# A tenth of the exponentials on VectorE, scores in rounds of four heads, one shared PSUM bank: attention with a gated feed-forward on one core

## The chip, the cores and the metric

The kernel runs on one core of a Trainium2 chip. The time is that of one execution in device microseconds, the median of three runs. One execution was also taken by the hardware profiler. A core has five engines that work through queues of their own and wait for one another by semaphores: TensorE (PE; PEld are its weight loads), VectorE (DVE), ScalarE (ACT), GpSimd (POOL) and SyncE (SP, which only starts transfers here). The on-chip memory SBUF and the matmul memory PSUM have 128 partitions. PSUM has eight banks of 512 fp32 columns.

## The reference: what is computed

The inputs are bf16: `x` (2048 × 640), `wqkv` (640 × 1920), `wo` (640 × 640), `w_gate` and `w_up` (640 × 1728), `w_down` (1728 × 640). With 32 heads of 20 columns:

```
xn = layernorm(x)
q, k, v = heads of xn @ wqkv                         # 32 heads, 20 columns
s  = concat over heads of softmax(q k^T / sqrt(20)) v   @ wo
h  = sigmoid(xn @ w_gate) * (xn @ w_up)              # 1728 columns
out = x + s * silu(h @ w_down)
```

The scores of a head are a 2048 × 2048 matrix, so that the whole softmax takes 32 × 2048 × 2048 exponentials. In banks of 128 keys × 512 queries these are 2048 banks. All the rest of the work is small beside that on ScalarE, but it is not on TensorE.

## The kernel before

**Setup (L133 to L308).** `x` is loaded, normalised (statistics on VectorE), transposed on TensorE into `xnT`; the first keys, values and queries are made. Weights are padded so that each head holds 32 columns, the 20 of the head and one at place 0 that carries constants. In `kT_all` that place is 1 (`e0`), and in the values `v_all` too, so that the matmul with the values also gives the softmax's denominator. In the queries it carries minus an upper bound of the scores: `q_abs` (L103) makes the absolute value of q from PSUM in two VectorE instructions, a copy to bf16 (L105) and a bitwise AND on it (L107), and a matmul with `bound` (L96, L97; made from the maxima of k, L100) sums it into place 0. So the exponential never overflows, and no maximum over the scores is taken.

**Passes and chunks.** The work is 32 passes, `steps`: four chunks of 512 queries, and for each the eight groups of four heads. A pass has 16 tiles of 128 keys × 4 heads = 64 banks of scores. `scores` (L631 to L641) makes one bank per matmul (L638): four heads sit in four row bands of 32 of the array. The banks are cut into chunks of three and two in turn, `scA` and `scB` in PSUM; ScalarE takes each chunk's exponential in one instruction (L680) and writes `pA` or `pB` in SBUF as bf16. `pv` (L647 to L667) multiplies two key tiles × four heads of probabilities with the values, eight matmuls (L661) into the one bank `oacc`, the heads in four column bands. At a pass's end `normalise` (L494) copies `oacc` out (`oev`, L497), and sends the denominators through DRAM to spread them over the partitions (L498, L505, L510 and four broadcasts L515, all in GpSimd's queue), with a reciprocal (L509) between; GpSimd multiplies (L520).

**The fill.** All other matmuls are cut into jobs that run between the scores: `k_job`, `v_job`, `q_job` for later passes (L336 to L363), `gateup_job` (L377) with its tanh on ScalarE (L396) and product on VectorE (L410), `down_job` (L415; copy L427, tanh L431, product L435), `out_job` (L460; L456 on VectorE, L458 on GpSimd), and `part_job` (L476). They share two banks, `misc`. sigmoid and silu are made from tanh.

**The order.** The program is written out in one order, and each engine's queue follows it. Per chunk the loop L675 to L706 emits the exponential, the tanhs and products that are due (`defer`, counted in chunks), the scores of the next chunk, a `pv` where it is due, and as much fill as fits: `room` is ScalarE's time for the chunk less TensorE's for the rest, at 216 ns per matmul of 512 columns (`MM`) and 100 ns per change of kind (`SWITCH`); `credit` grows by the work that is left over the chunks that are left (`quota`). PSUM: three banks `scA`, two `scB`, two `misc`, one `oacc`.

```
pt = wk.tile([P, n, 512], BF16, tag=("pA", "pB")[ci % 2], bufs=3, name=("pA", "pB")[ci % 2])
nc.scalar.activation(out=pt, in_=sc, func=ACT.Exp)
```

**The end (L709 to L764).** After the last exponential come the last `pv`, the last normalising by matmuls, the last two groups of `wo` and the stores.

Of the kernel before, what the change touches and what calls it, by code (L numbers as in the profile page):

```python
# [20 lines left out]
CHUNK = (3, 2)  # L21
# [3 lines left out]
def kernel(  # L25
# [24 lines left out]
    scale = float(Dh) ** -0.5  # L50
# [27 lines left out]
    v_all = persist.tile([P, TT, HEAD, 32], BF16, name="v_all")  # L78
# [5 lines left out]
    ep = early.enter_context(tc.tile_pool(name="early", bufs=1))  # L84
# [3 lines left out]
    def k_matmuls(ps, g, c):  # L88
        for kd in range(KD):
            nc.tensor.matmul(ps, lhsT=wkp[:, kd, GH * g:GH * g + GH, :].rearrange("p h e -> p (h e)"),  # L90
                             rhs=xnT[:, kd, c * 512:(c + 1) * 512],
                             start=(kd == 0), stop=(kd == KD - 1))
            yield
# [9 lines left out]
    def q_abs(ps):  # L103
        absq = wk.tile([P, QC], BF16, tag="absq", bufs=2, name="absq")
        nc.vector.tensor_copy(out=absq, in_=ps)  # L105
        bits = absq.bitcast(mybir.dt.uint16)
        nc.vector.tensor_scalar(out=bits, in0=bits, scalar1=0x7FFF, scalar2=None, op0=ALU.bitwise_and)  # L107
        return absq

    def v_matmuls(ps, tt, h):  # L110
        for kd in range(KD):
            nc.tensor.matmul(ps[:, 0:HALF], lhsT=xnT[:, kd, tt * P:(tt + 1) * P],  # L112
                             rhs=wv[:, kd, h * HALF:(h + 1) * HALF],
                             start=(kd == 0), stop=(kd == KD - 1))
            yield

    def v_dst(tt, h):
        return v_all[:, tt, h * HH:(h + 1) * HH, 1:1 + Dh]

    def q_matmuls(ps, qc, g):  # L120
        for kd in range(KD):
            nc.tensor.matmul(ps, lhsT=wqp[:, kd, GH * g:GH * g + GH, :].rearrange("p h e -> p (h e)"),  # L122
                             rhs=xnT[:, kd, qc * QC:(qc + 1) * QC],
# [8 lines left out]
    v_done = set()  # L132
    with tc.tile_pool(name="setup", bufs=1) as sp, \  # L133
# [29 lines left out]
        nc.vector.memset(v_all[:, :, 0:HH, 1 + Dh:32], 0.0)  # L163
# [7 lines left out]
        for j in range(GH):  # L171
            nc.gpsimd.memset(e0[32 * j:32 * j + 1, :], 1.0)
            nc.gpsimd.memset(esum[32 * j:32 * j + 32, 32 * j:32 * j + 1], -1.0)
# [41 lines left out]
        def k_mm(c):  # L215
            kps[c] = ps0.tile([P, 512], FP32, tag="k", bufs=2, name="ps_k")
            for _ in k_matmuls(kps[c], 0, c):
                pass
# [5 lines left out]
        def v_mm(t):  # L224
            vps[t] = ps0.tile([P, 512], FP32, tag="v", bufs=2, name="ps_v")
            for _ in v_matmuls(vps[t], t, 0):
                pass

        def v_evict(t):
            nc.scalar.activation(out=v_dst(t, 0), in_=vps[t][:, 0:HALF].rearrange("p (h e) -> p h e", e=Dh),  # L230
                                 func=ACT.Copy)
            v_done.add((t, 0))
# [3 lines left out]
        def q_mm():  # L236
            first["ps"] = ps0.tile([P, 512], FP32, tag="q", bufs=1, name="ps_q")
            for _ in q_matmuls(first["ps"], 0, 0):
# [6 lines left out]
        def q_evict():  # L245
            qT = wk.tile([P, QC], BF16, tag="qT", bufs=3, name="qT")
            nc.scalar.activation(out=qT, in_=first["ps"], func=ACT.Copy, scale=scale)
# [55 lines left out]
        nc.gpsimd.memset(v_all[:, :, HH:HEAD, 1 + Dh:32], 0.0)  # L303
# [9 lines left out]
    def misc(name):  # L313
        return psum.tile([P, 512], FP32, tag="misc", bufs=2, name=name)


    SWITCH, MM = 100.0, 216.0
    oTs = {}
    later = []
    slot = [0]  # L320

    def defer(n, fn):
        later.append((slot[0] + n, fn))

    def run_later(everything=False):
        while True:
            due = [x for x in later if everything or x[0] <= slot[0]]
            if not due:
                return
            for x in due:  # L330
                later.remove(x)
            for x in due:
                x[1]()


    def k_job(g, c):  # L336
        ps = misc("ps_k")
        for _ in k_matmuls(ps, g, c):
            yield MM
        dst = kT_all[:, g, c * 512:(c + 1) * 512]  # L340
        nc.vector.tensor_scalar(out=dst, in0=ps, scalar1=e0[:, 0:1], scalar2=None, op0=ALU.add)
        k_max(dst, g, c)
        if c == 3:
            k_bound(g)

    def v_job(tt, h):
        ps = misc("ps_v")
        for _ in v_matmuls(ps, tt, h):
            yield HALF / 2.4 + 3
        nc.vector.tensor_copy(out=v_dst(tt, h), in_=ps[:, 0:HALF].rearrange("p (h e) -> p h e", e=Dh))  # L350
        v_done.add((tt, h))

    def q_job(qc, g):
        ps = misc("ps_q")
        for _ in q_matmuls(ps, qc, g):
            yield MM
        absq = q_abs(ps)
        yield None
        nc.tensor.matmul(ps, lhsT=bound[:, g, :], rhs=absq, start=False, stop=True, skip_group_check=True)
        qT = wk.tile([P, QC], BF16, tag="qT", bufs=3, name="qT")  # L360
        nc.vector.tensor_scalar(out=qT, in0=ps, scalar1=scale, scalar2=None, op0=ALU.mult)
        qTs[qc, g] = qT
        yield MM  # L363
# [3 lines left out]
    def load_glu(c, kf):  # L367
        fsz, f0 = fsz_list[kf], kf * P
        wg = glu[0].tile([P, KD, P], BF16, tag="wg", bufs=3, name="wg")
        nc.sync.dma_start(out=wg[:, :, 0:fsz], in_=B_w_gate[:, f0:f0 + fsz].rearrange("(kd p) f -> p kd f", p=P))  # L370
        wu = glu[0].tile([P, KD, P], BF16, tag="wu", bufs=3, name="wu")
# [3 lines left out]
    hTs = {}  # L375

    def gateup_job(c, kf):  # L377
        fsz = fsz_list[kf]
        n = c * NFT + kf + 2
# [6 lines left out]
        t0 = c * QC  # L386
        psg = misc("psg")
        for kd in range(KD):
            nc.tensor.matmul(psg[0:fsz, :], lhsT=wg[:, kd, 0:fsz], rhs=xnT[:, kd, t0:t0 + QC],  # L389
                             start=(kd == 0), stop=(kd == KD - 1))  # L390
            yield MM
        tnh = wk.tile([P, QC], BF16, tag="tnh", bufs=2, name="tnh")
        done = []

        def gate():
# [397 lines left out]
```

## Time and profile before

| what | value |
|---|---|
| three runs | 1080.61, 1086.87, 1092.41 us; median 1086.87 |
| profiled execution | span 1079.7 us from the first to the last instruction; no other time is shown for it |
| mean granted TensorE clock | 0.929 |
| busy | PE 84%, ACT 92%, DVE 24%, POOL 22% of the span |
| first and last start of an exponential of the scores | 52.38 and 1050.96 us |
| chain that ended last | ACT 57%, issue 20%, PE 17%, DVE 5% |
| the two largest groups | L680 on `scA`, 410 times; L680 on `scB`, 409 times |

A row of groups names line, engine, operation, output and input with their shapes, how often, then busy us, the mean ns of one, and the engine's idle time just before them with what ended it. An ACT duration of 1590 ns for three banks does not mean that the next can start 1590 ns later: successive instructions overlap by some 0.25 us, and starts show the rate. PEclk is the clock that TensorE was granted, in tenths of full speed.

### The profile page before, as it was taken

What the parts mean: (1) busy time and instruction counts of PE and PEld (TensorE: products, weight loads), DVE (VectorE), ACT (ScalarE), POOL (GpSimd) and SP (SyncE); (2) the same over time, 40 slices, a digit from 0 to 9 for tenths busy, and PEclk for the clock granted to TensorE, in tenths of its full rate; (3) what the DMA queues carried; (4) which work ended last, traced back from release to release, by engine and by line L of the source; (5) the groups of instructions that cost most, each with busy time, mean ns of one, the idle gap of its engine ahead of it and who ended that gap; (6) DMA issues with size and microseconds to landing.
All of it is one profiled execution on the core that took longest, in us unless ns stands there. A gap on an engine that the chain in (4) does not pass through costs nothing.

```text
span 1079.7 us, 15225 instructions
## 1 busy us (share of the span) xinstructions
PE 906.9 (84%) x5968; PEld 295.3 (27%) x5968; DVE 259.3 (24%) x477; ACT 990.1 (92%) x934; POOL 232.5 (22%) x368
## 2 busy tenths in 40 slices
PE   4599999999998888888888987888887988889983
PEld 2232332322232322222321222222232332223332
DVE  7533444511122211111111111111111111111212
ACT  4497999999998999999988999999999999999990
POOL 6601111111122411111220321111111331111142
PEclk9798999999998999999965899889998999999995
DMA  5110000332111221111120212111011122210000
GB/s 188 26 30 12 11 12 9 111 73 65 36 54 66 67 54 39 43 39 30 42 66 14 65 42 48 42 42 41 27 60 41 42 67 54 48 32 12 12 23 24
DMA packets 92327, 48.79 MB, mean 45 GB/s; under 512 B 78724, under 2 KB 86820, under 8 KB 92256
## 3 DMA queue, kind: packets, MB, share of 16 engines
q1 hardware_dynamic: 83776, 33.03, 12.2%
q0 software_dynamic: 8480, 14.80, 4.5%
q8 instruction: 46, 0.75, 0.3%
q14 instruction: 25, 0.20, 0.1%
HBM read 40.74 MB, written 7.06 MB: 44 GB/s over the span
## 4 chain that ended last, share of the span: by engine, by line
ACT 57%; issue 20%; PE 17%; DVE 5%; POOL 0%; POOLq 0%; ACTq 0%; DVEq 0%
ACT pA L680 27%; ACT pB L680 24%; ACT tnh L396 4%; PE scA L638 3%; PE scB L638 3%; PE oacc L661 2%; PE psd L424 2%; PE psg L389 2%; ACT td L431 1%; DVE stats L187 1%; PE ps_v L112 1%; DVE absq L107 1%; PE pss L467 1%; PE psu L403 1%; PE ps_k L90 1%
## 5 line engine op out<-in xcount | busy, mean ns | idle before, releaser
L680 ACT ACTIVATE pA<-scA 128x1536 bf16<-128x1536 f32 x410 | 652.0, 1590 | 24.8 <-PE scA L638 24.6
L680 ACT ACTIVATE pB<-scB 128x1024 bf16<-128x1024 f32 x409 | 476.0, 1164 | 8.1 <-PE oacc L661 5.1
L638 PEld LDWEIGHTS <-kT_all 32*128 32x128 bf16 x2048 | 119.9, 91 | 376.4 <-issue 354.4
L638 PE MATMUL scB<-qT,kT_all 32*128 32x512 bf16 x818 | 170.9, 398 | 57.3 <-ACT pB L680 43.7
L638 PE MATMUL scA<-qT,kT_all 32*128 32x512 bf16 x1230 | 168.4, 399 | 48.4 <-ACT pA L680 37.8
L661 PE MATMUL oacc<-pA,v_all 128*32 128x512 bf16 x1230 | 167.3, 407 | 1.0 <-ACT pA L680 1.0
L661 PE MATMUL oacc<-pB,v_all 128*32 128x512 bf16 x818 | 165.7, 407 | 0.2 <-ACT pB L680 0.2
L498 POOL DMA_DIRECT2D den_dram<-oev x31 | 18.2, 588 | 476.1 <-DVE oev L497 476.1
L410 DVE SCALAR_TENSOR_TENSOR hT<-tnh,psu 128x512 bf16<-128x512 bf16 (+1 forms) x56 | 38.4, 686 | 275.7 <-PE psu L403 139.2
L424 PE MATMUL psd<-wd,hT 128*128 128x320 bf16 x448 | 99.0, 323 | 0.5 <-ACT tnh L396 0.5
L389 PE MATMUL psg<-xnT,wg 128*128 128x512 bf16 (+1 forms) x280 | 93.9, 399 | 4.9 <-ACT tnh L396 4.9
L403 PE MATMUL psu<-xnT,wu 128*128 128x512 bf16 (+1 forms) x280 | 86.7, 391 | 0.0
L515 POOL DMA_DIRECT2D rl<-rec_dram x124 | 61.5, 501 | 48.0 <-DMA rec_dram<-den 45.0
L122 PE MATMUL ps_q<-xnT,wqp 128*128 128x512 bf16 x160 | 52.2, 400 | 1.4 <-ACT tnh L396 1.4
L424 PEld LDWEIGHTS <-hT 128*128 128x128 bf16 x448 | 34.0, 100 | 69.9 <-issue 60.3
L520 POOL TENSOR_TENSOR oT<-oev,rl 128x512 bf16<-128x512 f32 x31 | 39.2, 1264 | 58.8 <-DMA rl<-rec_dram 50.9
L661 PEld LDWEIGHTS <-v_all 128*32 128x32 bf16 x2048 | 31.4, 95 | 68.1 <-issue 68.1
L90 PE MATMUL ps_k<-xnT,wkp 128*128 128x512 bf16 x160 | 48.4, 391 | 1.5 <-DVE mk_all L100 1.4
L427 DVE COPY d<-psd 128x320 f32<-128x320 f32 x32 | 15.7, 491 | 129.2 <-PE psd L424 129.2
L497 DVE COPY oev<-oacc 128x512 f32<-128x512 f32 x31 | 21.4, 692 | 100.7 <-PE oacc L661 100.6
L467 PE MATMUL pss<-wo_pad,oT 128*128 128x320 bf16 x192 | 42.4, 325 | 0.0
L396 ACT ACTIVATE tnh<-psg 128x512 bf16<-128x512 f32 (+1 forms) x56 | 40.9, 731 | 0.0
(97 smaller groups left out, 532.9 us busy)
## 6 DMA issues: line engine op xcount, KB each, us to landing
wg<-in_B_w_gate_dram SPq DMA_DIRECT2D x52, 160.0 KB
wu<-in_B_w_up_dram SPq DMA_DIRECT2D x52, 160.0 KB
rl<-rec_dram POOLq DMA_DIRECT2D x124, 64.0 KB, 2.3
gq_dram<-d POOLq DMA_DIRECT2D x12, 320.0 KB, 2.4
gqr<-gq_dram SPq DMA_DIRECT2D x12, 320.0 KB
xr<-in_A_x_dram SPq DMA_DIRECT2D x16, 160.0 KB
wd<-in_B_w_down_dram SPq DMA_DIRECT2D x1, 2080.0 KB
out_dram<-ot POOLq DMA_DIRECT2D x12, 160.0 KB, 2.7
```

What stands on the lines that cost most here:

```text
L90: nc.tensor.matmul(ps, lhsT=wkp[:, kd, GH * g:GH * g + GH, :].rearrange("p h e -> p (h e)"), rhs=xnT[:, kd, c * 512:(c + 1) * 512], start= ...
L122: nc.tensor.matmul(ps, lhsT=wqp[:, kd, GH * g:GH * g + GH, :].rearrange("p h e -> p (h e)"), rhs=xnT[:, kd, qc * QC:(qc + 1) * QC], start= ...
L389: nc.tensor.matmul(psg[0:fsz, :], lhsT=wg[:, kd, 0:fsz], rhs=xnT[:, kd, t0:t0 + QC], start=(kd == 0), stop=(kd == KD - 1))
L396: nc.scalar.activation(out=tnh[0:fsz, :], in_=psg[0:fsz, :], func=ACT.Tanh, scale=0.5)
L403: nc.tensor.matmul(psu[0:fsz, :], lhsT=wu[:, kd, 0:fsz], rhs=xnT[:, kd, t0:t0 + QC], start=(kd == 0), stop=(kd == KD - 1))
L424: nc.tensor.matmul(psd[:, 0:HALF], lhsT=hT[0:fsz, kf, t4 * P:(t4 + 1) * P], rhs=glu[1][0:fsz, kf, e0_:e1_], start=(kf == 0), stop=(kf == N ...
L467: nc.tensor.matmul(pss[:, 0:HALF], lhsT=oTs[qc, g][:, t4 * P:(t4 + 1) * P], rhs=wo_pad[:, g, h * HALF:(h + 1) * HALF], start=(g == 0), sto ...
L515: nc.gpsimd.dma_start(out=rl[32 * j:32 * j + 32, :], in_=rec_dram[n, j:j + 1, :].to_broadcast([32, QC]))
L520: nc.gpsimd.tensor_tensor(out=oT, in0=oev, in1=rl, op=ALU.mult)
L638: nc.tensor.matmul(sc[:, i, :], lhsT=kT_all[32 * j:32 * j + 32, g, kt * P:(kt + 1) * P], rhs=qTs[qc, g][32 * j:32 * j + 32, :], start=True ...
L661: nc.tensor.matmul(oaccs[p][32 * j:32 * j + 32, :], lhsT=v_all[:, kt, GH * g + j, :], rhs=where.pop(n), start=(kt == 0), stop=(kt == KT - ...
L680: nc.scalar.activation(out=pt, in_=sc, func=ACT.Exp)
```

## The change

- **Exponentials.** Scores come in rounds of one key tile × four heads. Three pairs of PSUM banks (`sc0` to `sc2`) form a ring; round r takes the pairs 2r mod 3 and 2r+1 mod 3. ScalarE takes a pair at a time (`pP`, 811 times). In 213 rounds the first pair is split: ScalarE takes one bank (`pS`), VectorE the other in five instructions.
- **The exponential on VectorE.** The queries are scaled by log2(e)·2^23 besides 1/sqrt(20), so a score, with an offset added and rounded to an integer, already is the bit pattern of a power of two with a linear mantissa. `bits` reads PSUM, adds the offset, clamps and writes int32; `mantissa` takes the mantissa's bits as a number from 1 to 2; `square` and `cube` make a cubic of it by Horner's rule, and `power` multiplies it with the first number. ScalarE's exponential undoes the factor by its `scale`.
- **One miscellaneous bank.** `mbank` replaces the two `misc` banks. k, v, gate and up jobs take half of it (256 columns), the others the whole of it; a k or gate-and-up job is done in two halves, so tanh and product become 112 of 256 columns instead of 56 of 512.
- **The order** is made by a planner that keeps a clock for TensorE (`pe`) and queues with clocks for ScalarE and VectorE (`act`, `dve`): each task has a duration, cells of times that it depends on, and a rank. The loop issues the next round when its banks come free or when ScalarE is about to run dry, and otherwise a `pv` batch or fill.
- **Smaller edits.** `q_abs` reads the high halves of the fp32 values in PSUM in one instruction. `v_all` has 22 places per head instead of 32, a PV matmul takes 21 columns, and the memsets of the padding go (L163 on VectorE, L303 on GpSimd). The later values are made in pieces of 12, 12 and 8 heads. `oev` and `rl` have one buffer instead of two, `wg` and `wu` two instead of three. `esum` holds −1.015625 instead of −1.

```diff
-        nc.vector.tensor_copy(out=absq, in_=ps)
-        bits = absq.bitcast(mybir.dt.uint16)
-        nc.vector.tensor_scalar(out=bits, in0=bits, scalar1=0x7FFF, scalar2=None, op0=ALU.bitwise_and)
+        high = ps.bitcast(U16).rearrange("p (q two) -> p q two", two=2)[:, :, 1]
+        nc.vector.tensor_scalar(out=absq.bitcast(U16), in0=high, scalar1=0x7FFF, scalar2=None,
+                                op0=ALU.bitwise_and)
...
-    def misc(name):
-        return psum.tile([P, 512], FP32, tag="misc", bufs=2, name=name)
-    SWITCH, MM = 100.0, 216.0
+    MM5, MM3 = 216.0, 136.0
+    INTO = {"score": 160.0, "pv": 100.0, "fill": 100.0}
+    PE_OUT, SEM = 260.0, 70.0
+    EXP_COL, EXP_FIX, EXP_LAG = 1 / 1.2, 52.0, 260.0
+    DMA_WAIT = 3400.0
...
+    AHEAD, HELD = 80.0, 20
+    mbank = psum.tile([P, QC], FP32, tag="misc", bufs=1, name="mbank")
+    def take_bank(whole):
+        ready = [i for i in range(2) if halves[i].t is not None and halves[i].t <= pe[0]]
+        if whole and len(ready) == 2:
+            halves[:] = [Cell(), Cell()]
+            return (0, 1), mbank
+        if not whole and ready:
+            i = min(ready, key=lambda i: halves[i].t)
+            halves[i] = Cell()
+            return (i,), mbank[:, i * HC:(i + 1) * HC]
+        return None
...
+    PAIRS, SINGLES, DKEEP, D_BACKLOG = 8, 3, 4, 3000.0
...
+    def act_exp(ps, r, heads, begun):
...
+            nc.scalar.activation(out=buf.tile(PAIRS if n == 2 else SINGLES), in_=ps, func=ACT.Exp, scale=exp_scale)
...
+    def dve_exp(ps, r, j, begun):
+        def bits():
+            t["e"] = pp.tile([P, 512], I32, tag="de", bufs=2, name="de")
+            nc.vector.tensor_scalar(out=t["e"], in0=ps, scalar1=BITS0, scalar2=-2.0 ** 31, op0=ALU.add, op1=ALU.max)
+        def mantissa():
+            t["m"] = pp.tile([P, 512], I32, tag="dm", bufs=1, name="dm")
+            nc.vector.tensor_scalar(out=t["m"], in0=t["e"], scalar1=0x7FFFFF, scalar2=0x3F800000,
+                                    op0=ALU.bitwise_and, op1=ALU.bitwise_or)
+        def square():
+            t["u"] = pp.tile([P, 512], FP32, tag="du", bufs=1, name="du")
+            m = t["m"].bitcast(FP32)
+            nc.vector.scalar_tensor_tensor(out=t["u"], in0=m, scalar=C2, in1=m, op0=ALU.add, op1=ALU.mult)
+        def cube():
+            nc.vector.scalar_tensor_tensor(out=t["u"], in0=t["u"], scalar=C1, in1=t["m"].bitcast(FP32),
+                                           op0=ALU.add, op1=ALU.mult)
+        def power():
+            nc.vector.scalar_tensor_tensor(out=buf.tile(DKEEP)[:, 0, :], in0=t["u"], scalar=C0,
+                                           in1=t["e"].bitcast(FP32), op0=ALU.add, op1=ALU.mult)
+        first = dve.add(600.0, [Cell(begun + MM5 + PE_OUT - 100.0), *d_made[-2:-1]], bits, -2)
+        c = dve.add(340.0, [first, *d_made[-1:]], mantissa, 3)
+        c = dve.add(590.0, [c], square, 3)
+        c = dve.add(590.0, [c], cube, 3)
+        buf.made = dve.add(590.0, [c, buf.before], power, 3)
...
+    def issue():
+        r = rounds[0]
+        kt = r % PASS_ROUNDS
+        first, second = (2 * r) % 3, (2 * r + 1) % 3
+        pe_do("score", 0.0)
+        begun = pe[0]
+        split = (r > 1 and kt < PASS_ROUNDS - 3 and dve.backlog + max(0.0, dve.t - pe[0]) < D_BACKLOG
+                 and all(c.t is not None for c in d_made[-2:-1]))
+        order = [(kt + i) % GH for i in range(GH)]
...
+        if split:
+            slots[first] = [act_exp(tiles[0][:, 0:1, :], r, order[0:1], begun),
+                            dve_exp(tiles[0][:, 1, :], r, order[1], begun)]
+        else:
+            slots[first] = [act_exp(tiles[0], r, order[0:2], begun)]
+        slots[second] = [act_exp(tiles[1], r, order[2:4], begun)]
+        pe_do("score", MM5 + 12.0)
...
+            free = max(c.t if c.t is not None else guess for c in cells)
+            dry = max(act.t, pe[0]) + sum(t[2] for t in act.queue) - MM5 - PE_OUT + 2000.0 * stuck
+            into = 0.0 if mode[0] == "score" else INTO["score"]
+            until = max(free, dry - AHEAD) - into
...
-    for ci, (b0, n) in enumerate(chunks):
-        nc.scalar.activation(out=pt, in_=sc, func=ACT.Exp)
...
+    while pv_pass[0] < len(steps):
+        advance(pe[0])
```

## The prediction

> **What bounds the kernel now.** I read the engine totals first, then the 40 slices, then the groups.
>
> ```profile
> PE 906.9 (84%) x5968; PEld 295.3 (27%) x5968; DVE 259.3 (24%) x477; ACT 990.1 (92%) x934; POOL 232.5 (22%) x368
> ...
> ACT  4497999999998999999988999999999999999990
> ...
> PEclk9798999999998999999965899889998999999995
> ...
> L680 ACT ACTIVATE pA<-scA 128x1536 bf16<-128x1536 f32 x410 | 652.0, 1590 | 24.8 <-PE scA L638 24.6
> L680 ACT ACTIVATE pB<-scB 128x1024 bf16<-128x1024 f32 x409 | 476.0, 1164 | 8.1 <-PE oacc L661 5.1
> ```
>
> ScalarE (ACT) is busy in nearly every slice from the third to the last but one, and its exponentials (L680) waited only 33 us in all. The slices where it drops to 8 are those where PEclk drops. Durations of pipelined instructions overlap, so the price of one is the distance between starts when nothing waits (columns: start, duration, instruction):
>
> ```profile
> 204.14 1.28 ACT L680 ACTIVATE pB<-scB 128x1024 bf16<-128x1024 f32 x1
> 205.05 1.71 ACT L680 ACTIVATE pA<-scA 128x1536 bf16<-128x1536 f32 x1
> 206.40 1.28 ACT L680 ACTIVATE pB<-scB 128x1024 bf16<-128x1024 f32 x1
> ...
> 223.70 0.62 ACT L396 ACTIVATE tnh<-psg 128x512 bf16<-128x512 f32 x1
> 224.18 1.05 ACT L680 ACTIVATE pB<-scB 128x1024 bf16<-128x1024 f32 x1
> ```
>
> Two banks take 0.905 us, three 1.331 to 1.35, a 512-column tanh 0.478; a tanh of 640 takes 0.622. So 409×1.331 + 409×0.905 + 56×0.478 + 16×0.622 = 951 us. The loop runs from the first exponential at 52.4 to the end of the last at about 1051, 998.6 us; 47 us are stalls. Of these 38 lie in gaps over 0.5 us, in stretches of low clock (columns: window, its length, busy us of PE, PEld, DVE, ACT, POOL, then the granted clock):
>
> ```profile
> 540.00:542.00 2.00, 1.15 (x7) 0.55 (x7) 0.75 (x1) 2.00 (x3) 0.59 (x1) 1.00 0.00 0
> 542.00:544.00 2.00, 1.32 (x14) 0.35 (x13) 0.00 (x0) 2.00 (x3) 0.00 (x0) 0.87 0.40 164
> 544.00:546.00 2.00, 2.00 (x11) 0.44 (x7) 0.49 (x1) 1.46 (x3) 0.00 (x0) 0.50 0.66 192
> ...
> 560.00:570.00 10.00, 10.00 (x52) 2.25 (x51) 1.18 (x2) 7.23 (x8) 2.79 (x5) 0.53 0.30 93
> 570.00:580.00 10.00, 9.48 (x49) 2.10 (x51) 0.00 (x0) 7.83 (x7) 0.00 (x0) 0.50 0.00 0
> ```
>
> After a few us of light TensorE work the clock falls to 0.50; TensorE is then full, ACT is busy 72 to 78% and waits. I count 12 such falls in the loop, 3.2 us each.
>
> The Trainium skill, "TensorE: Matmul & The Clock Gate", section "What's actually happening", says that full clock comes back after one busy window of about 3.4 us. The trace differs: TensorE stays 95 to 100% busy at 0.50 to 0.53 for the 20 us shown. By the rule 12 falls would last one window each and cost, as an estimate, 12 × 3.4 × 0.25 = 10 us, and the sum below would be 22 us lower; by the rows they cost 38, and I go by these.
>
> **The change part by part.**
>
> *ScalarE.* 213 of 2048 banks go to VectorE. What remains: 811 pairs × 0.905 + 213 singles × 0.478 (the tanh row has the same 512 columns) + 112 half-width tanhs × 0.265 (0.478 less 256 columns at (1.331−0.905)/512 = 0.83 ns) + 16×0.622 = 734 + 102 + 30 + 10 = **875.5 us, 75.8 less**. Cutting threes into pairs costs fixed time; it is in this sum.
>
> *VectorE* becomes a heavy user. Rows:
>
> ```profile
> L497 DVE COPY oev<-oacc 128x512 f32<-128x512 f32 x31 | 21.4, 692 | 100.7 <-PE oacc L661 100.6
> L435 DVE SCALAR_TENSOR_TENSOR d<-td,d 128x640 f32<-128x640 bf16 x12 | 9.9, 825 | 29.3 <-ACT td L431 29.3
> ...
> 80.45 0.68 DVE L105 CAST absq<-ps_q 128x512 bf16<-128x512 f32 x1
> 81.16 0.29 DVE L107 TENSOR_SCALAR absq<-absq 128x512 uint16<-128x512 uint16 x1
> ...
> 34.21 9.21 DVE L107 TENSOR_SCALAR absq<-absq 128x512 uint16<-128x512 uint16 x1
> 38.76 4.36 POOL L304 MEMSET wo_pad<- 128x5120 bf16 x1
> ```
>
> A split is bits 0.692 (PSUM read, as L497), mantissa 0.29 to 0.69 (I take 0.43, the 128x512 f32 broadcast copy of the tail, L740), three two-operand steps of 512/640 × 0.825, about 0.69: 3.19 us, 680 in all. The other VectorE work between first and last split adds about 218: 112 tanh products of 256 columns and 55 halves of k at 0.42 (the tail's 128x256 product, L750), 93 instructions of 512 columns for q and `oev` at 0.69, 27 maxima at 0.69, 33 of v at 0.41, 63 of 320 columns at 0.49, 16 × 0.825, 31 reciprocals × 0.25. In its order 1106 neighbours are independent (83 ns overlap each) and 401 dependent (34 ns more, as 80.45 to 81.16): 680 + 218 − 92 + 14 = **about 820 us**, under ACT's 875 but not far.
>
> *The coupling.* In the built program both readers of a split pair are ordered. In 156 of 213 splits bits waits for ACT's single exponential; in 56 ACT waits for bits. Behind bits, 158 score matmuls wait, and behind those all of TensorE's queue.
> First case: the single ends 0.48 after its start S, bits near S + 1.39; from a score matmul's start to its exponential's is 0.5 us (219.62 to 220.12), while ACT has two or three instructions in hand. Stepping the order of rounds (splits follow each other 36 times) gives 22 us of ACT stall if VectorE is on time, 36 if 150 ns late, 55 at 300, 76 at 450. VectorE is occupied by steps of 0.69 about 85% of the time, and bits goes first among what is ready: I take **36**.
> Second case: 56 × 0 to 0.44; I take 0.3, **17**.
>
> *One miscellaneous bank in two halves.* 110 of 112 tanhs wait for the last matmul into the other half; 79 matmuls wait mid-group for the other half's reader. The tanh sits in ACT's queue, exponentials behind it. 110 × 0 to 0.3 us (at most one streaming of the half, plus the semaphore); I take 0.1, as fill is spread between rounds: **11**. The stalls outside low clock stay at **9**.
>
> *TensorE.* The same streams: fill about 300 us before and after, PV 1 column band narrower without saving time, but the four scores of a round stream side by side and runs of one kind fall from 1672 to 1277. Streaming and switches together go from about 590 to 526 us, 0.62 and 0.60 of ACT's work. A fall therefore costs slightly less, 2.7 us. Their number: windows of 3.4 us with too little row-weighted streaming were 6 in the order of before and 5 to 12 after; by time in use 11, and about 30. I keep 12: **32 us** (bounds 13 and 100).
>
> *Setup and its queues.* The absolute value of q was a copy (L105) and L107; L107 took 9.21 us at 34.21, against 0.29 elsewhere, while GpSimd (POOL) ran memsets to 43.4, and the first exponential followed it. Now it is one PSUM read, but `bound` (L97) still works in SBUF beside the same memsets: gain 0 to 9.7, I take half, **4.6**: front 47.8.
> The Trainium skill, "SBUF — State Buffer", section "Who interferes with whom", has VectorE and GpSimd share a port pair that one holds for a whole instruction. The row of 9.21 us agrees, and the rule speaks against the change: its two-operand steps can meet the 31 multiplies of L520, 1.26 us each. By it VectorE would carry up to 39 us more, 860, and the sum would still be ACT's.
> The `wg`/`wu` loads (SP's queue) are now one deep; the first waits behind the 2080 KB of `wd`, 0 to 6 us once, of fill that others cover. The normalising chain (POOL's queue: one store, one load, one store, four broadcasts) with one buffer ends 13 to 21 us into a pass of 27 or more: nothing, but if it exceeded the pass, each pass would wait. Tail: 28.7 before, 0 to 2 more, **29.3**.
>
> **Sum.** 47.8 + 875.5 + 36 + 17 + 11 + 9 + 32 + 29.3 = 1057.6 us, against a span of 1079.7 that lies 0.9 under the fastest of three runs; their median is 7.2 above the span. So 1057.6 + 7.2 = **1065 us**, 2% faster. What is late next: TensorE's queue behind bits.
>
> **The rivals.**
> 1. *ACT's bound nearly reached*, with stalls of 45 to 75 in all instead of 105: 47.8 + 875.5 + 45 to 75 + 29.3 + 7.2 = 1005 to 1035. For it: in an unsplit round the second pair comes free 0.4 us before ACT needs it. Against: the orderings above.
> 2. *VectorE becomes the bound*: mantissa at 0.69 adds 213 × 0.26 = 55, and being held up in SBUF, as in the row of 9.21 us, during the 31 multiplies of GpSimd (L520, 1264 ns each) 39 more: 914. It also waits for ACT and TensorE in its order, 70 to 90 us if each coupling above costs it what it costs ACT: a loop of 985 to 1005, with 47.8 + 29.3 + 7.2 a time of 1070 to 1090, no change. For it: VectorE's own load is within 60 us of ACT's. Against: the busy time of L107 is 294 ns in the loop, unhindered.
> 3. *Slower: the clock.* Rounds stream four bands at once, so TensorE is idle longer between them. If windows count by time in use, 35 falls × 2.9 = 100 in place of 32: 1133 us. It decides from about 20 falls on, a loop clock near 0.88.
> 4. *The change does not save what it says*: VectorE 450 ns late or more, every split giving back its 0.43 us: 76 + 25 + 33 + 9 + 32 = 175 of stalls, 1135 us.
>
> **How the numbers follow.** Forecast (1035 to 1095) 0.47; rival 1, 0.18; rival 2, 0.10; rival 3, 0.14; rival 4, 0.11. A measurement here can tell about 1% from no change (1076 to 1098). Faster: 0.34 of the forecast's 0.47, 0.18, and 0.02 of rival 2: 0.54. Same: 0.12 and 0.07: 0.19. Slower: 0.25, and 0.02 of the others: 0.27. The range reaches from rival 1's floor near 1005 to 1120, part of the way into rivals 3 and 4, whose cores lie beyond it (about 0.17).
>
> **What the next profile would show.** ACT's starts in full-clock stretches: 0.905 and 0.478 apart. Waits of scores on the bits step: 30 to 50 us of ACT idle; over 70 is rival 4. VectorE busy near 80% with mantissa at 0.43. PEclk with about 12 falls; 20 or more is rival 3. First exponential near 48. I am wrong if VectorE's order, not its load, holds TensorE, or if full-clock stalls are near zero.

## The result and the profile after

The changed kernel takes **1121.9 us** (median of four runs, 1120.0 to 1129.3) against 1087.4 for the kernel before: a ratio of 1.034, with a 95% interval of 1.027 to 1.041. In a later comparison it was 1.039 (1.034 to 1.044). It is slower; the forecast was 1065. The profiled execution of the changed kernel is the slowest of its four (1129.3 us), so sums over its trace lie some 7 us above the median.

The first lines of its page, to be laid beside those of the kernel before (engine totals, then ACT, the clock and the chain that ended last):

```profile
PE 887.7 (79%) x6715; PEld 358.9 (32%) x6748; DVE 893.6 (79%) x1610; ACT 939.0 (83%) x1195; POOL 243.6 (22%) x367
...
ACT  4599889989889885899887887999979887889781
...
PEclk9799899999989997999989887999988998999986
...
DVE 34%; PE 32%; ACT 21%; issue 10%; POOL 1%; DMA 1%; POOLq 0%; DVEq 0%; ACTq 0%
```

ScalarE is no longer full anywhere for long, VectorE is at 79%, and the chain of work that ended last, which was ScalarE's for 57%, is now spread over VectorE, TensorE and ScalarE. No engine is the bound; they wait for one another. What ScalarE waited for stands in its own groups (after the second bar: idle us before these instructions, and what ended it):

```profile
L873 ACT ACTIVATE pP<-sc 128x1024 bf16<-128x1024 f32 x811 | 787.7, 1041 | 33.1 <-PE sc L849 31.6
L873 ACT ACTIVATE pS<-sc 128x512 bf16<-128x512 f32 x213 | 129.5, 608 | 68.9 <-DVE de L884 31.9 <-PE sc L849 23.9 <-PE oacc L968 12.3
L503 ACT ACTIVATE tnh<-mbank 128x256 bf16<-128x256 f32 (+1 forms) x112 | 43.7, 391 | 31.7 <-PE mbank L509 29.5 <-DVE du L894 1.3
```

The single exponentials of the split rounds (`pS`) have the longest idle time though they are a fifth of the exponentials; half of it is ended by VectorE's first step (`de`, L884), a third by scores. The halved tanhs, which never waited before (0.0 at L396), now wait 32 us for matmuls into the shared bank.

For all kernels here I made one ledger from the trace: from the first exponential to the end of the last, each ScalarE instruction at the price that the prediction used (0.905 us for a pair, 0.478 for a single, 0.265 for a half tanh, 0.622 for the tanh of 640 columns; before, 1.33 for three banks), and all beyond that between two starts counted as stall, at full clock or next to a stretch of half clock (a "fall").

| | before | changed | predicted |
|---|---|---|---|
| front, to the first exponential | 52.4 | 49.0 | 47.8 |
| ScalarE's work | 952.6 | 875.1 | 875.5 |
| stalls at full clock | 10.6 | 120.9 | 73 |
| stalls at half clock (falls of the clock) | 36.7 (12) | 57.8 (34) | 32 (12) |
| tail | 27.4 | 24.7 | 29.3 |
| span | 1079.7 | 1127.5 | 1057.6 |

The work in this ledger is the count of instructions at the forecast's own prices, so that it agrees is no surprise. What the trace adds is that the prices hold: where nothing waits, starts are again 0.905, 0.478 and 0.264 us apart. The stalls took the gain back, and 54 us more than that in the loop: 178.7 us of them, where 105 were allowed. How they divide between the two rows of stalls depends on what is called next to a fall: counted by any overlap in time the changed kernel has 103 and 76; the sum stays.

One round of the changed kernel shows the loop of waits. First TensorE (start, duration, instruction, idle time before it and what ended that), then VectorE and ScalarE in the same 3 us:

```profile
205.88 0.27 PE L102 MATMUL mbank<-xnT,wkp 128*128 128x256 bf16 x1 [0.57 <-DVE kT_all L428]
...
206.62 0.40 PE L849 MATMUL sc<-qT,kT_all 32*128 32x512 bf16 x4
...
208.43 0.39 PE L849 MATMUL sc<-qT,kT_all 32*128 32x512 bf16 x2 [0.44 <-ACT pS L873]
```

```profile
205.34 0.48 DVE L428 TENSOR_SCALAR kT_all<-mbank,e 128x256 bf16<-128x256 f32 x1 [0.35 <-PE mbank L102]
205.74 0.42 DVE L888 TENSOR_SCALAR dm<-de 128x512 int32<-128x512 int32 x1
206.19 0.69 DVE L894 SCALAR_TENSOR_TENSOR du<-dm 128x512 f32<-128x512 f32 x1
207.05 0.69 DVE L884 TENSOR_SCALAR de<-sc 128x512 int32<-128x512 f32 x1 [0.17 <-PE sc L849]
```

```profile
207.78 0.60 ACT L873 ACTIVATE pS<-sc 128x512 bf16<-128x512 f32 x1 [0.99 <-DVE de L884]
208.27 4.68 ACT L873 ACTIVATE pP<-sc 128x1024 bf16<-128x1024 f32 x5
```

A matmul of the next keys waits for VectorE to empty a half of the shared bank; the scores stand behind it in TensorE's queue; VectorE's first step waits for the scores; ScalarE's single exponential waits for that step, as both read the same pair, and idles 0.99 us; and the next scores into the pair wait for the single.

### The profile page after: what moved, and what is told of

It is laid out like the page before. It is cut to its first block, busy times and chain, and to the rows that moved or that the text cites. A ratio compares the mean times of both kernels' runs of the same rounds, so it can differ in the third digit from the quotient of the medians.

```text
span 1127.5 us, 17969 instructions
## 1 busy us (share of the span) xinstructions
PE 887.7 (79%) x6715; PEld 358.9 (32%) x6748; DVE 893.6 (79%) x1610; ACT 939.0 (83%) x1195; POOL 243.6 (22%) x367
## 4 chain that ended last, share of the span: by engine, by line
DVE 34%; PE 32%; ACT 21%; issue 10%; POOL 1%; DMA 1%; POOLq 0%; DVEq 0%; ACTq 0%
ACT pP L873 11%; DVE de L884 8%; PE sc L849 8%; ACT pS L873 7%; DVE du L897 5%; PE oacc L968 5%; PE mbank L509 4%; DVE du L894 4%; PE mbank L496 4%; PE mbank L531 3%; DVE dp L901 3%; ACT tnh L503 3%; DVE dm L888 2%; PE mbank L102 2%; DVE hT L513 2%
## 5 line engine op out<-in xcount | busy, mean ns | idle before, releaser
L873 ACT ACTIVATE pP<-sc 128x1024 bf16<-128x1024 f32 x811 | 787.7, 1041 | 33.1 <-PE sc L849 31.6
L849 PE MATMUL sc<-qT,kT_all 32*128 32x512 bf16 x2048 | 305.2, 405 | 77.7 <-DVE de L884 50.1
L884 DVE TENSOR_SCALAR de<-sc 128x512 int32<-128x512 f32 x213 | 146.7, 689 | 90.4 <-ACT pS L873 69.9
L873 ACT ACTIVATE pS<-sc 128x512 bf16<-128x512 f32 x213 | 129.5, 608 | 68.9 <-DVE de L884 31.9
L968 PE MATMUL oacc<-pP,v_all 128*21 128x512 bf16 x1622 | 181.1, 409 | 0.2 <-ACT pP L873 0.2
L897 DVE SCALAR_TENSOR_TENSOR du<-du,dm 128x512 f32<-128x512 f32 x213 | 158.1, 742 | 4.1
L901 DVE SCALAR_TENSOR_TENSOR dp<-du,de 128x512 bf16<-128x512 f32 x213 | 151.5, 711 | 4.6
L894 DVE SCALAR_TENSOR_TENSOR du<-dm 128x512 f32<-128x512 f32 x213 | 150.4, 706 | 3.5
L496 PE MATMUL mbank<-xnT,wg 128*128 128x256 bf16 (+1 forms) x560 | 97.4, 286 | 31.7 <-DVE hT L513 17.6
L968 PE MATMUL oacc<-dp,v_all 128*21 128x512 bf16 x213 | 84.2, 409 | 25.3 <-DVE dp L901 23.7
L509 PE MATMUL mbank<-xnT,wu 128*128 128x256 bf16 (+1 forms) x560 | 93.0, 285 | 13.5 <-ACT tnh L503 7.6
L888 DVE TENSOR_SCALAR dm<-de 128x512 int32<-128x512 int32 x213 | 100.0, 469 | 0.9
```

Of the source, the lines that this page charges most:

```text
L509: nc.tensor.matmul(psu[0:fsz, :], lhsT=wu[:, kd, 0:fsz], rhs=xnT[:, kd, cols], start=(kd == 0), stop=(kd == KD - 1))
L849: nc.tensor.matmul(ps, lhsT=kT_all[32 * j:32 * j + 32, g, kt * P:(kt + 1) * P], rhs=qTs[qc, g][32 * j:32 * j + 32, :], start=True, stop=Tr ...
L873: nc.scalar.activation(out=buf.tile(PAIRS if n == 2 else SINGLES), in_=ps, func=ACT.Exp, scale=exp_scale)
L884: nc.vector.tensor_scalar(out=t["e"], in0=ps, scalar1=BITS0, scalar2=-2.0 ** 31, op0=ALU.add, op1=ALU.max)
L888: nc.vector.tensor_scalar(out=t["m"], in0=t["e"], scalar1=0x7FFFFF, scalar2=0x3F800000, op0=ALU.bitwise_and, op1=ALU.bitwise_or)
L894: nc.vector.scalar_tensor_tensor(out=t["u"], in0=m, scalar=C2, in1=m, op0=ALU.add, op1=ALU.mult)
```

## The experiments

**Without splits.**

```diff
-    PAIRS, SINGLES, DKEEP, D_BACKLOG = 8, 3, 4, 3000.0
+    PAIRS, SINGLES, DKEEP, D_BACKLOG = 8, 3, 4, -1.0
```

> The changed kernel with no bank given to VectorE: 1024 pairs on ScalarE, the ring, the planner and the one bank as they are. ScalarE's work rises from 875 to 966 us (1024 x 0.905 + 112 x 0.265 + 16 x 0.622). Theory A (the stalls of 179 us come mostly from the split pairs, in which VectorE waits for ScalarE's single exponential, the next scores for VectorE, and ScalarE for the scores): stalls fall to 60 to 85 us, so 49 + 966 + 60 to 85 + 27 = 1102 to 1127 us, about the same time as with the splits. Rival B (the stalls come from the planner's order and the one bank, whatever the splits): stalls stay at 160 to 179, about 1200 us.

Measured: 1111.4 us, 1.032 of the kernel before (1.029 to 1.034). Work 966.0, stalls 67.6 us (49.8 at full clock), 17 falls. So rival B is out for most of the stalls: the 213 splits save ScalarE 91 us and bring 111 us of stalls in the two profiled executions, or 93 to 99 us by the medians. But even without splits the kernel is slower than the one before, by 13 us more work (pairs in place of threes, halved tanhs) and by 50 us of full-clock stalls against 10.6, for the ring, the planner and the one bank together. What its two largest groups on ScalarE waited for:

```profile
L873 ACT ACTIVATE pP<-sc 128x1024 bf16<-128x1024 f32 x1024 | 966.9, 1165 | 19.4 <-PE sc L849 18.5
L503 ACT ACTIVATE tnh<-mbank 128x256 bf16<-128x256 f32 (+1 forms) x112 | 51.1, 456 | 25.1 <-PE mbank L509 24.5 <-PE mbank L496 0.4
```

**A shorter chain on VectorE.**

```diff
         def mantissa():
-            ...
+            pass
         def square():
-            ...
+            pass
         def cube():
-            ...
+            pass
         def power():
-            nc.vector.scalar_tensor_tensor(out=buf.tile(DKEEP)[:, 0, :], in0=t["u"], scalar=C0, ...
+            nc.vector.tensor_copy(out=buf.tile(DKEEP)[:, 0, :], in_=t["e"].bitcast(FP32))
```

> Leaves out three of VectorE's five instructions per split bank (mantissa, square, cube), and the last is a plain copy of the first one's bits, so these exponentials are only piecewise linear; order and splits are planned as before. VectorE loses about 213 x 2.06 = 440 us of work. Theory A (the ordering inside the split pair, between engines that are not full): 0 to 25 us less than the changed kernel, 1097 to 1122. Rival C (VectorE's load and its lateness): most of the full-clock stalls go, 1020 to 1060.

Measured: 1056.1 us, 0.981 of the kernel before. Stalls 110.0, 17 falls. The time lies in rival C's range and theory A's is missed: 428 us less busy time of VectorE take away 69 us of the 179 in the ledger, about 60 by the medians. But not most of the full-clock stalls went, as rival C said: some 81 us of them are left. In all 42 us more are left than without splits, though VectorE is at 44%, which points to the order inside a split.

**The tanh without the bank.**

```diff
-                nc.scalar.activation(out=made["t"][0:fsz, :], in_=psg[0:fsz, :], func=ACT.Tanh, scale=0.5)
+                nc.scalar.activation(out=made["t"][0:fsz, :], in_=xnT[0:fsz, 0, cols], func=ACT.Tanh, scale=0.5)
```

> The 112 tanhs of the gate read 256 columns of xnT in SBUF in place of the gate's bank, so the gate is left out of the result; every other instruction stays. They no longer wait for the matmuls into the other half of the one bank, nor hold that bank. If the 37 us that ScalarE waits there add to the time: 1085. If the waits only move to the next link (scores, split pairs): 1105 to 1122.

Measured: 1107.2 us, 1.028 of the kernel before (1.026 to 1.030), so by the two measurements of the changed kernel some 6 to 12 us less than it. The tanh's idle time went to 0.0; ScalarE's waits for scores and for VectorE's first step grew from 87 to 97 us. The second reading is nearer: with splits, most of this wait does not come back as time.

**The single bank last.** In a split round ScalarE takes the other pair first.

```diff
-            slots[first] = [act_exp(tiles[0][:, 0:1, :], r, order[0:1], begun),
-                            dve_exp(tiles[0][:, 1, :], r, order[1], begun)]
...
+            bits = dve_exp(tiles[0][:, 1, :], r, order[1], begun)
+            slots[second] = [act_exp(tiles[1], r, order[2:4], begun)]
+            slots[first] = [act_exp(tiles[0][:, 0:1, :], r, order[0:1], begun, bits), bits]
...
+        split = (r > 1 and len(d_made) < 214 * r / ROUNDS and kt < PASS_ROUNDS - 3
...
+        yield "known", lambda: (c, kf) in glu_w and len(glu_done) >= c * NFT + kf
```

> The same number of splits (213), but in a split round ScalarE takes the round's other pair first and its single bank after VectorE's first instruction, so VectorE never waits for ScalarE inside a pair, and ScalarE has 0.9 us of other work while VectorE reads. (A gate-and-up job also starts only when the one before it is through its matmuls.) Theory A: the waits of VectorE on the single exponential (70 us) and of ScalarE on VectorE's first instruction (32 us) go, 60 to 100 us less: 1022 to 1062. Rival C (load): within 1% of the changed kernel, 1110 to 1133.

Measured: 1155.5 us, 1.075 of the kernel before, worse than the changed kernel. Both theories missed. The waits named did go (VectorE's on the single left its list), and another came:

```profile
L875 ACT ACTIVATE pP<-sc 128x1024 bf16<-128x1024 f32 x811 | 784.4, 1035 | 99.9 <-PE sc L851 97.5
L875 ACT ACTIVATE pS<-sc 128x512 bf16<-128x512 f32 x213 | 129.4, 607 | 21.9 <-DVE de L886 20.8
```

I had overlooked the ring. The first pair of a round is the second of the next, and the next round's four scores go out as one group. When the single comes last, these scores wait for it (82 us in all, against 10 in the changed kernel), and ScalarE has nothing in hand while they are made, about half a us in each of 213 rounds. So the price of a split is paid at the moment at which the pair that the next round needs comes free. That gave the next edit.

**The split in the second pair**, which the ring needs one round later.

```diff
-            slots[first] = [act_exp(tiles[0][:, 0:1, :], r, order[0:1], begun),
-                            dve_exp(tiles[0][:, 1, :], r, order[1], begun)]
-        else:
-            slots[first] = [act_exp(tiles[0], r, order[0:2], begun)]
-        slots[second] = [act_exp(tiles[1], r, order[2:4], begun)]
+            slots[first] = [act_exp(tiles[0], r, order[0:2], begun)]
+            slots[second] = [act_exp(tiles[1][:, 0:1, :], r, order[2:3], begun),
+                             dve_exp(tiles[1][:, 1, :], r, order[3], begun)]
+        else:
+            slots[first] = [act_exp(tiles[0], r, order[0:2], begun)]
+            slots[second] = [act_exp(tiles[1], r, order[2:4], begun)]
```

With it go the same cap on the number of splits (213) and the same rule for the gate-and-up jobs. Put alone into the changed kernel, these two leave its program as it is, instruction for instruction; here the cap only keeps the number of splits at 213, where it would be 222.

> 213 splits again, but of the round's second pair, which the ring needs one round later than the first: ScalarE takes the first pair, then its single bank, while VectorE reads the other bank 0.9 us earlier than ScalarE gets to the pair. (A gate-and-up job starts only when the one before it is through its matmuls.) If the order inside the split rounds costs the 42 us of stalls that the short chain still had more than the kernel without splits: 20 to 45 us less than the changed kernel, 1069 to 1094. If VectorE's load sets the rest alone: 1103 to 1125.

Beside it ran the changed kernel once more, a quadratic, and half the splits (the cap line with 107 in place of 214, and nothing else):

> The changed kernel once more, beside the other three on one chip, so that they can be compared with it. By its ratio to the kernel before (1.034) and the 1077.7 us that the kernel before took in the last comparison: about 1114 us.

> The cubic becomes a quadratic (one of the five VectorE instructions less per split; its greatest relative error is 0.34% in place of 0.07%), the order and the splits are planned as before. VectorE loses 213 x 0.61 = 130 us and some 12 us of long instructions. The short chain took 440 us away and gained 58 us against 1114. If the gain is proportional to the load: 18 us, 1096. If the stalls come from VectorE queueing near its limit, the first relief is worth most: 30 to 45 us, 1069 to 1084. If only the order matters: 1110 to 1118.

> Half as many splits (107), spread evenly. ScalarE's work is 920 us. If stalls go linearly with the splits, from 68 us at none to 179 at 213: 123, a time of 49 + 920 + 123 + 27 = 1119, no change. If they grow faster near VectorE's limit: 85 to 100, 1081 to 1096, better than both none and 213.

The quadratic's edit, with the planner still reserving the cube's time, so that order and splits stay:

```diff
-C2, C1, C0, LOG2_LEAD = -6.64634996, 12.93906117, -16.68093785, -3.23180960
+B1, B0, LOG2_LEAD = -2.97052671, 6.23476810, -2.09726611
-BITS0 = (127.0 + LOG2_LEAD) * OCTAVE - 2.0 ** 31
+BITS0 = (127.0 + LOG2_LEAD) * OCTAVE
...
         def cube():
-            nc.vector.scalar_tensor_tensor(out=t["u"], in0=t["u"], scalar=C1, ...
+            pass
```

Measured, all on one chip (the kernel before 1081.0): the changed kernel 1123.9, 10 more than was expected; the split of the second pair **1074.3**, a ratio of 0.994 (0.991 to 0.996); the quadratic **1083.0**, 1.003 (1.0005 to 1.006); half the splits 1102.9, 1.020 (1.013 to 1.027).

- The second pair gains 50 us at the same VectorE load (its chain instructions take the same time). ScalarE's stalls fall from 179 to 124. VectorE no longer waits for the single exponential, and the scores no longer for VectorE's first step:

```profile
L886 DVE TENSOR_SCALAR de<-sc 128x512 int32<-128x512 f32 x213 | 145.8, 684 | 46.0 <-PE sc L851 43.5 <-ACT pS L875 1.2
...
L851 PE MATMUL sc<-qT,kT_all 32*128 32x512 bf16 x2048 | 304.9, 395 | 65.2 <-ACT pP L875 56.1
```

against these lines of the changed kernel:

```profile
L884 DVE TENSOR_SCALAR de<-sc 128x512 int32<-128x512 f32 x213 | 146.7, 689 | 90.4 <-ACT pS L873 69.9 <-PE sc L849 18.4
...
L849 PE MATMUL sc<-qT,kT_all 32*128 32x512 bf16 x2048 | 305.2, 405 | 77.7 <-DVE de L884 50.1
```

- The quadratic gains 41 us for 144 us of VectorE time, at the same order; the short chain had gained about 60 for 428. The first relief is worth most, as the second reading (VectorE queueing near its limit) said. Yet VectorE's wait for the single exponential did not shrink with it, it grew, from 70 to 122 us (to 217 with the short chain). What shrank is a wait at the chain's other end: the matmuls with the values waited 23.7 us for VectorE's result in the changed kernel, and here

```profile
L884 DVE TENSOR_SCALAR de<-sc 128x512 int32<-128x512 f32 x213 | 146.9, 690 | 142.5 <-ACT pS L873 121.8
...
L967 PE MATMUL oacc<-dp,v_all 128*21 128x512 bf16 x213 | 82.6, 399 | 3.8 <-DVE dp L900 3.7
```

- Half the splits: stalls 103, work 920, 21 us less than with all of them and also less than with none (1.032), but above the 1081 to 1096 of the better case and still slower than the kernel before.

**Both, the late tanh, and the buffers.** The tanh's edit moves its place in ScalarE's order behind the up matmuls that it has to wait for:

```diff
-            gated = act.add(270.0, [Cell(pe[0] + PE_OUT + 100.0), *tnh_free[-4:-3]], gate, 0, EXP_LAG)
-            give_bank(held, gated)
+            first_half, free4 = held, tnh_free[-4:-3]
             held, psu = yield "bank", False
             ...
                 yield "mm", MMH
+            gated = act.add(270.0, [Cell(pe[0] + PE_OUT + 100.0), *free4], gate, 0, EXP_LAG)
+            give_bank(first_half, gated)
```

and that of the buffers:

```diff
-OBUFS, WB = 1, 2
+OBUFS, WB = 2, 2
-    PAIRS, SINGLES, DKEEP, D_BACKLOG = 8, 3, 4, 3000.0
+    PAIRS, SINGLES, DKEEP, D_BACKLOG = 6, 3, 4, 3000.0
```

> Both changes that helped: the quadratic (41 us less than the changed kernel's 1124) and the split of the second pair (50 us less), 213 splits. If they act on different stalls they add: 1033. If both relieve the same loop (VectorE's first instruction in time for the ring), the second brings little: 1050 to 1066. The stalls of the kernel without splits, 68 us, would give 49 + 875 + 68 + 27 = 1019 as the floor.

> The kernel that splits the second pair (1074), with the gate's tanh put in ScalarE's order only after the up matmuls into the other half of the one bank are out, as it has to wait for them anyway. If the wait behind the one bank costs what ScalarE stood there (22 us in that kernel): 1050 to 1057. If holding the half longer starves TensorE's fill instead: 1074 or more.

> The changed kernel with two buffers for oev and rl, as before the change, and six buffers for the pairs of probabilities instead of eight, to make room. In the changed kernel one pass end stood 12.3 us for the multiply that reads the only oev buffer. If that is all that the single buffers cost: 10 to 14 us less, 1110 to 1114. If six pairs are too few: no gain, or a loss.

> Quadratic, split of the second pair, late tanh, two oev and rl buffers and six pairs, together. If the gains add on top of the quadratic with the split of the second pair: 20 to 30 us less than that kernel, 1020 to 1040, faster than the kernel before by 4 to 6%.

Measured (the kernel before 1080.2):

| kernel | us | ratio (95%) | stalls, full + half clock | falls |
|---|---|---|---|---|
| quadratic and second pair | 1046.5 | 0.968 (0.962 to 0.973) | 69.7 + 27.5 | 15 |
| second pair, late tanh | 1068.1 | 0.987 (0.982 to 0.993) | 81.0 + 31.6 | 19 |
| changed kernel, two `oev`/`rl` and six pairs | 1129.5 | 1.045 (1.039 to 1.051) | 126.4 + 47.9 | 26 |
| all four | **1026.0** | **0.948** (0.941 to 0.955) | 58.2 + 13.5 | 7 |

The quadratic and the second pair gained 41 and 50 us, and together 77 of the possible 91: they act on overlapping stalls, but mostly add. (Here the planner no longer reserves the cube's time, so the order is a new one too.) The late tanh gained 6 us where 17 to 24 were expected: its wait fell from 21 to 3 us, and the waits of the pairs for scores rose from 34 to 46 us. The half of the bank is held longer: matmuls into the bank waited 71 us for the product on VectorE that frees it, where it had been 34. The buffers did not pay in the changed kernel: the one stall of 12.3 us is gone, but a new wait stands in ScalarE's group, for the probabilities' buffers that the `oacc` matmuls release, which points to six pairs being too few there. The kernel was also planned anew, and the two effects were not told apart.

```profile
L873 ACT ACTIVATE pP<-sc 128x1024 bf16<-128x1024 f32 x810 | 789.8, 1038 | 55.2 <-PE oacc L968 26.8 <-PE sc L849 26.1
```

All four together beat both kernels:

```profile
PE 828.1 (81%) x6715; PEld 350.1 (34%) x6748; DVE 750.0 (73%) x1397; ACT 928.5 (91%) x1195; POOL 239.7 (23%) x367
...
ACT  4599999899999998999999999999999899999980
...
PEclk9799999999999999999999999999998899999995
```

ScalarE is full again in nearly every slice, with the same 875 us of work as in the changed kernel, and the clock falls 7 times. Late tanh and buffers together gained 20 us on top of the quadratic and the second pair, where each had brought 6 us or nothing elsewhere; which of them does it was not run.

## Why the prediction was wrong, point by point

- **ScalarE's work**: 875.5 forecast, 875.1 in the ledger, with the prices confirmed by the distances between starts. Right. (The sum of before took 409 instructions of three banks for the 410 of the row, 951 us for 952.6.)
- **Front and tail**: 47.8 and 29.3 forecast, 49.0 and 24.7 measured. The first exponential came 3.4 us earlier than before instead of 4.6. The forecast's tail began at the last exponential's start, not its end, which counts 0.9 us of work twice.
- **VectorE's load**: about 820 us forecast; from the first split to the last it was occupied for 852, mantissa near 0.42 as taken. The difference is 32 us of chain steps that took longer than usual (below), which the sum left to rival 2.
- **The coupling is the step that failed.** It stood in the sum with 36 us for VectorE 150 ns late and 17 for ScalarE waiting for the first step, 53 together, and the clock's falls stayed at 12, as if the splits added none. The splits brought 111 us of stalls (178.7 less the 67.6 without them; 93 to 99 by the medians), of which 71 at full clock, with the 12 of the one pass end below among them, and 40 next to falls, of which they added 17. The price was worked out for one round with VectorE's lateness as a free number, and added to the clock as if the two had nothing to do with each other. VectorE was not late in that sense: in 156 splits its first step came after the single exponential, at the median 33 ns after its end, and it stood 70 us at the head of its queue waiting for ScalarE. That wait alone is not the price either, since it grew to 122 and 217 us in two faster kernels. What the runs show in its place are two parts. One is the order: the scores of the next round waited 50 us for VectorE's first step, and 68 with either shorter chain, so this does not fall with the load; it left the list when the split moved to the second pair, and the time fell by 50 us. That is the sign of being wrong that the prediction had named itself ("VectorE's order, not its load"). The other is the load all the same: with one instruction less per split, at the same order, the time fell by 41 us, and the 24 us for which TensorE had waited at the chain's end went to 4. How the falls and the other stalls divide between cause and effect stays open.
- **The one bank** and the rest of the new order: 11 us forecast for the tanhs and 9 for all else at full clock; without splits there were 50 at full clock, and the tanhs alone stood some 33 us in all (about 40 with splits). Of the range "110 × 0 to 0.3" the upper end was right. Taking the wait away gave back only 6 to 12 us while the splits were as they were.
- **The single buffers**: priced at nothing, "if it exceeded the pass, each pass would wait". One pass end did: at 448.6 us ScalarE stood for 12.3 us. The only `oev` buffer waited for the multiply L663, which stood in GpSimd's queue behind the last output rows (L574, L593), as the order of time in all engines shows:

```profile
444.41 0.79 POOL L574 TENSOR_TENSOR ot<-gqr,xr 128x320 bf16<-128x320 f32 x1 [1.71 <-DVE gqr L572]
445.50 0.56 POOL L593 DMA_DIRECT2D out_dram<-ot  x1 [0.30 <-POOL ot L574]
446.08 1.27 POOL L663 TENSOR_TENSOR oT<-oev,rl 128x512 bf16<-128x512 f32 x1
447.39 0.69 DVE L637 COPY oev<-oacc 128x512 f32<-128x512 f32 x1 [3.05 <-POOL oT L663]
448.13 0.38 PE L968 MATMUL oacc<-pS,v_all 128*21 128x512 bf16 x1 [1.87 <-DVE oev L637]
...
448.60 0.60 ACT L873 ACTIVATE pS<-sc 128x512 bf16<-128x512 f32 x1 [12.33 <-PE oacc L968]
```

- **The clock**: I kept 12 falls at 2.7 us, 32; there were 34 at 1.7, 57.8 (2.2 and 76 by overlap). Rival 3's count (35) came true, but by luck as far as the traces tell. The prediction weighed two counts. Take the windows of 3.41 us on whose edges the granted clock changes, and add up in each the time in which matmuls stream (0.21 us for 512 columns, twice that at half clock), weighted with the share of the 128 rows in use: a quarter for one score, the whole for four side by side. A window at full clock with less than 0.37 of its length, the limit that fits these traces, is followed by half clock, one with more is not: this holds for 259 of 260 windows before, 256 of 264 in the changed kernel and 267 of 267 with the second pair. Time in use without the weight, with its best limit, 0.45, gives 257, 246 and 260. So the traces speak against rival 3's way of counting, and for the one whose forecast was 5 to 12 falls; that was made for the planned order, without the stalls that left TensorE less to stream. With the same matmuls there were 15 falls with the quadratic, 18 with the second pair, 7 in the last kernel.
- **The rivals**: the time ended short of rivals 3 (1133) and 4 (1135, "the change does not save what it says"). What rival 4 says is what the kernel without splits showed: 1111 us, no slower than with them. Its mechanism, VectorE 450 ns late, was not it: a lateness over 0.15 us after the single's end was seen in 18 of 213 splits, 11 us in all. Rival 2, VectorE as the bound, was not it either: 144 us less of its work gave 41 us, and 428 gave about 60. The range ended at 1120 and left rivals 3 and 4 to the 2 in 10, though stalls and falls rose together (17 falls without splits, 34 with them); counted as one case of more stalls it would have had to be inside.
- **The rule on the clock** (the Trainium skill, "TensorE: Matmul & The Clock Gate", section "What's actually happening"), which I set aside for the rows of before: in the changed kernel 27 of 34 falls lasted one window of 3.4 us, as it says; before, 2 of 12 did. By the weighted count above, and a limit of 0.72 fitted likewise, a window at half clock with more is followed by full clock and one with less by half clock, in 43 of 44 windows of the changed kernel and 28 of 32 before; that scores now come in fours would make the difference, but no run changed that alone.

What stays open: whether the order of two readers of one pair alone, without the ring, costs anything. In the kernel with the second pair VectorE's step comes first in 212 of 213 rounds, so both changed at once. Open is also how much of a gain came by way of the clock, and how the 50 us of stalls without splits divide between the ring, the planner and the one bank.

## What to carry to other kernels

When work is moved from a full engine to an idle one, price the wait at the head of each in-order queue and the work that stands behind it, not only the load: here the splits saved ScalarE 91 us and brought 93 to 111 us of stalls, and the scores of the next round stood 50 us behind an instruction that itself had waited for the engine that was to be relieved. In a ring, try to give the second reader the buffer that is needed last, and after that shorten its chain; these two steps turned 3% slower into 3% faster here, with not one exponential more or less on VectorE. In this kernel three engines are each about 80% busy in fixed order, and the terms that the sum had priced apart (coupling, one bank, clock) all came out higher; a range for such a case should reach as far as all of them together.

## What the runs showed of the hardware

VectorE's two-operand steps and its integer step, 0.42 to 0.69 us otherwise, took 1.0 to 2.0 us in 42 of the 852 steps behind the first, each time with GpSimd running an elementwise instruction. Two rows of the changed kernel, VectorE's and GpSimd's:

```profile
430.39 1.17 DVE L901 SCALAR_TENSOR_TENSOR dp<-du,de 128x512 bf16<-128x512 f32 x1
```

```profile
429.84 1.17 POOL L574 TENSOR_TENSOR ot<-gqr,xr 128x320 bf16<-128x320 f32 x1 [4.56 <-DVE gqr L572]
```

The step ends 0.55 us after GpSimd's does, having started 0.62 us before that end; a usual one takes 0.69. All the long two-operand steps end 0.55 us after GpSimd's instruction, all the long integer steps 0.28 to 0.30. Over the 213 splits the time beyond the usual was 32 us. The Trainium skill, "SBUF — State Buffer", section "Who interferes with whom", has such a pair of instructions exclude each other for their whole length; these rows agree, and the 39 us that the prediction named as an estimate for the multiplies was near. The first step, which reads PSUM, showed nothing of it (673 to 693 ns in all 213).
